# An adaLN block with memory attention and a gated FFN: deferred steps placed by an emission clock, and a new order of loads, Wo and norms

## The chip, the cores and the metric

The kernel runs on one core of a Trainium2 chip. The metric is device time in microseconds (us) of one execution; the time of a kernel is the median of its runs. A core has TensorE (PE in the profile: matmuls and transposes, which write to PSUM), VectorE (DVE), ScalarE (ACT), GpSimd (POOL) and SyncE (SP). Each works through its own instructions in program order, and an instruction waits on semaphores until what it reads is there and the buffer that it writes is free. Transfers are issued from the queues of SP and ACT and are carried out by 16 DMA engines that all queues share.

## The reference

The input x is 2048 tokens by 448, in bf16. A conditioning row c gives six rows of modulation, each 448 long. With the constants written out, what is computed is

```python
mod = silu(c) @ w_mod                      # sa, ca, ga, sb, cb, gb
h = layernorm(x) * (1 + ca) + sa
x = x + ga * attn(h)                       # 16 heads of 28, then @ wo
h = layernorm(x) * (1 + cb) + sb
x = x + gb * ((sigmoid(h @ w_gate) * (h @ w_up)) @ w_down)   # 1792 wide
```

The attention goes over the tokens in four segments of 512. Inside a segment it is causal softmax attention. Beside it stands a memory: with phi(t) = t + 1 for t > 0 and exp(t) otherwise, the output of a head is (1 - g) times the softmax result plus g times phi(q) M / (phi(q) z), where M and z sum phi(k) v and phi(k) over all earlier segments, and g is the sigmoid of a learnt number for each head. The first segment has no memory.

## The kernel before

A segment has four tiles of 128 tokens. Heads are handled in four groups of four (`hc`), and a *unit* is one segment and one group. `logits` (L370) computes a unit's transposed logits in three steps (`g` = 0, 1, 2), with an exponential on ACT and a causal mask on POOL behind each; `pv` (L395) multiplies with v and, from the second segment on, with the memory, and combines the two on DVE and POOL; `otr` (L441) transposes the result by DMA. Everything else is *fill*: jobs put between these steps to keep TensorE busy.

The order of all instructions is written out by hand, in one Python program; nothing is reordered later. The main loop (L583) goes over segments, groups and steps. After each `logits`, `run_fill` (L520) takes jobs from the queue `fill` until their listed costs, in ns of TensorE at full clock (a matmul of 512 columns counts 216, of 448 columns 190), reach a quota. What a job overspends is carried as debt.

The jobs are: q, k and v projections (`proj_qk` L308, `proj_v` L319); `mem_k` (L341: phi of k and a DMA transpose to `pk`) and `mem_update` (L350: 16 matmuls and the new memory); `wo_tile` (L450: output projection of a tile, the residual, and LN2's statistics); `modulate` of LN2 (L259); `gate_up` (L466), 14 for each segment; `down` (L481), four for each segment; and the preparations `prep_b1` to `prep_b3` (L528), which multiply ga into wo and gb into w_down on POOL and compute the second norm's modulation columns.

Steps that need another engine to finish first are deferred: `later(n, fn)` emits fn after n *ticks*, and a tick is one job or one attention step, whatever its length (L73 to L88). phi (L330) puts its exponential on ACT at once and its two DVE operations two ticks later. A layer norm of a segment (`class LN`, L232) runs statistics on DVE, a power on POOL, the normalisation on DVE, four DMA transposes from SP and four modulations on DVE. For segment 0 the transposes are done by TensorE (`pe_chunk`, L264), and the modulation takes the data out of PSUM. For LN1 of segments 1 to 3 its steps are jobs of cost 0, blended one by one between the projections of the segment before (`ln1_jobs` L277, `blend` L289).

SP carries the loads of x, of most modulation matrices, wq, wv and wo, all DMA transposes and the stores. ACT's queue carries the loads of w_gate, w_up and w_down, blended between the projections of segment 0 (`ffn_load_jobs` L146). POOL clears the unused rows of wo, w_gate and w_up at the beginning (`late_loads` L132). A tile of PSUM for matmul results comes from a ring of four banks (`ps_m`); the logits have the other four.

When segment s - 1's last `otr` is out (segment s, group 0), the four `wo_tile` jobs of s - 1 are put in front of the fill, and behind it `down` of s - 2, the modulations of LN2 and the gate/up jobs of s - 1 (L594 to L600). The last segment's gate, up and down run at the end with nothing to interleave.

## Time and profile before

| | us |
|---|---|
| median of three runs | 325.17 (323.58 to 325.18) |
| profiled execution, its own time | 324.38 |
| its span, first to last instruction | 322.4 |
| TensorE busy | 267.0 (83% of the span) |
| VectorE busy | 184.2 (57%) |
| ScalarE busy | 141.7 (44%) |
| GpSimd busy | 105.9 (33%) |
| mean granted TensorE clock | 0.91 of full speed |

Times in the profile count from the first instruction. A busy TensorE is not a fast one: its clock is granted between half and full speed, and four matmuls of 512 columns take 0.86 us at full clock, so the same work is longer where the clock is low. In a row of the timeline, the bracket at the end is the idle time of the engine just before the instruction and what ended it. A line number such as L261 is that of the kernel before; a helper has one line for all who call it.

### The profile page before, as it was taken

The page shows a single profiled execution, that of the slowest core. Times are in us where ns is not written, and L with a number is a line of the kernel's source. Part 1 is how long each engine was busy: PE and PEld are TensorE (multiplying, and loading weights), DVE is VectorE, ACT ScalarE, POOL GpSimd, SP SyncE. Part 2 cuts the span into 40 slices and gives each one's busy share as a digit, 9 for nine tenths or more (in the row PEclk, how much of TensorE's full clock was granted, in tenths as well). Part 3 has the DMA queues.
Part 4 walks back from the last instruction along what each step waited for, and adds up shares of the span by engine and source line. Part 5 has one row for each costly group of instructions (what it writes and reads, how often), then busy time and mean ns, then how long its engine had stood idle before and what let it go on. Part 6 is the DMA issues. An engine that isn't in the chain of part 4 may idle for free.

```text
span 322.4 us, 5232 instructions
## 1 busy us (share of the span) xinstructions
PE 267.0 (83%) x2032; PEld 126.3 (39%) x2032; DVE 184.2 (57%) x403; ACT 141.7 (44%) x171; POOL 105.9 (33%) x162
## 2 busy tenths in 40 slices
PE   6679029959779639999599599989959999989996
PEld 2424004516334303445145154435514554534452
DVE  4846365489496952763484455469562754743421
ACT  1237305855866505576603357763436521023310
POOL 0808100636359780322443030435431310400000
PEclk9969657989999957999679799999968999999999
DMA  6978990234631110000012100001310001210001
GB/s 172 290 167 259 229 234 9 50 78 88 116 67 36 42 40 0 18 2 16 18 44 64 33 16 3 16 18 33 95 31 2 16 2 32 63 47 0 0 16 43
DMA packets 43088, 20.18 MB, mean 63 GB/s; under 512 B 31800, under 2 KB 42168, under 8 KB 43064
## 3 DMA queue, kind: packets, MB, share of 16 engines
q1 hardware_dynamic: 39016, 14.01, 19.6%
q10 hardware_dynamic: 4048, 5.85, 5.9%
q8 instruction: 16, 0.26, 0.3%
q14 instruction: 8, 0.07, 0.1%
HBM read 10.67 MB, written 1.84 MB: 39 GB/s over the span
## 4 chain that ended last, share of the span: by engine, by line
PE 52%; DVE 23%; DMA 9%; ACT 6%; POOL 5%; issue 3%; SPq 1%; POOLq 0%; ACTq 0%; DVEq 0%
PE gps L471 14%; PE ups L476 14%; PE dps L484 11%; ACT pT L386 5%; DMA hT<-xn 5%; PE pq L312 4%; DVE xn L250 4%; DVE hT L261 3%; PE acc L405 3%; DVE st L242 3%; PE lg L383 3%; PE pwo L453 3%; DMA pk<-pkt 2%; DVE e L335 2%; DVE pkt L336 2%
## 5 line engine op out<-in xcount | busy, mean ns | idle before, releaser
L386 ACT ACTIVATE pT<-lg 128x2048 bf16<-128x2048 f32 (+1 forms) x48 | 76.5, 1593 | 56.9 <-PE lg L383 54.4
L471 PE MATMUL gps<-hT,wg_sb 128*128 128x512 bf16 x224 | 63.5, 400 | 14.9 <-DVE hT L261 14.1
L479 DVE SCALAR_TENSOR_TENSOR fT<-tt,ups 128x512 bf16<-128x512 f32 x56 | 38.4, 686 | 61.6 <-PE ups L476 45.7
L392 POOL TENSOR_SCALAR_AFFINE_SELECT pT<-pT 128x512 bf16<-128x512 bf16 x64 | 39.9, 641 | 69.8 <-ACT pT L386 66.3
L473 ACT ACTIVATE tt<-gps 128x512 f32<-128x512 f32 x56 | 32.8, 596 | 67.1 <-PE gps L471 67.1
L476 PE MATMUL ups<-hT,wu_sb 128*128 128x512 bf16 x224 | 60.3, 393 | 0.0
L484 PE MATMUL dps<-wd_sb,fT 128*128 128x448 bf16 x224 | 44.4, 354 | 0.0
L471 PEld LDWEIGHTS <-wg_sb 128*128 128x128 bf16 x224 | 20.8, 100 | 43.9 <-issue 17.1
L312 PE MATMUL pq<-hT,wq_sb 128*128 128x512 bf16 x64 | 20.8, 437 | 18.8 <-DVE hT L261 18.8
L476 PEld LDWEIGHTS <-wu_sb 128*128 128x128 bf16 x224 | 22.5, 101 | 29.8 <-issue 5.4
L439 POOL TENSOR_TENSOR ou<-t,t 128x448 bf16<-128x448 f32 x12 | 13.8, 1147 | 60.1 <-DVE t L438 52.7
L484 PEld LDWEIGHTS <-fT 128*128 128x128 bf16 x224 | 21.7, 98 | 21.0 <-issue 1.5
L383 PE MATMUL lg<-qT,kT 28*128 28x512 bf16 (+3 forms) x256 | 17.9, 312 | 5.6 <-ACT pT L386 4.2
L261 DVE TENSOR_SCALAR hT<-hT,cols 128x512 bf16<-128x512 bf16 x28 | 14.5, 564 | 12.6 <-DMA hT<-xn 12.6
L488 DVE TENSOR_TENSOR ot<-dps,x_sb 128x448 bf16<-128x448 f32 x16 | 10.0, 622 | 19.8 <-PE dps L484 18.8
L250 DVE TENSOR_SCALAR xn<-x_sb,mv,rs 128x448 bf16<-128x448 bf16 x32 | 16.8, 545 | 6.5 <-POOL rs L247 6.5
L242 DVE BATCH_NORM_STATS2 st<-x_sb 128x6 f32<-128x448 bf16 x32 | 19.7, 617 | 1.3 <-DMA x_sb<-in_A_x_dram 0.7
L312 PE MATMUL pq<-hT,wk_sb 128*128 128x512 bf16 x64 | 19.3, 430 | 0.9 <-DVE kT L317 0.9
L405 PEld LDWEIGHTS <-pT 128*128 128x128 bf16 x640 | 18.3, 96 | 4.0 <-issue 0.8
L405 PE MATMUL acc<-vt,pT 128*128 128x29 bf16 x640 | 18.5, 175 | 0.6 <-ACT qT L315 0.6
L541 POOL TENSOR_TENSOR wd_sb<-wd_sb,gb 128x448 bf16<-128x448 bf16 x14 | 15.4, 1111 | 6.4 <-ACT gb L225 6.4
L453 PE MATMUL pwo<-wo_sb,oT 128*128 128x448 bf16 x64 | 16.1, 409 | 0.9 <-DMA oT<-ou 0.8
(82 smaller groups left out, 251.9 us busy)
## 6 DMA issues: line engine op xcount, KB each, us to landing
wm<-in_w_mod_dram SPq DMA_DIRECT2D x5, 392.0 KB, 4.9
out_dram<-ot SPq DMA_DIRECT2D x16, 112.0 KB, 1.7
wd_sb<-in_B_w_down_dram ACTq DMA_DIRECT2D x1, 1568.0 KB
x_sb<-in_A_x_dram SPq DMA_DIRECT2D x3, 448.0 KB, 6.1
wg_sb<-in_B_w_gate_dram ACTq DMA_DIRECT2D x3, 448.0 KB, 4.0
wu_sb<-in_B_w_up_dram ACTq DMA_DIRECT2D x3, 448.0 KB, 6.7
hT<-xn SPq DMA_TRANSPOSE x28, 2.3
wm<-in_w_mod_dram ACTq DMA_DIRECT2D x1, 392.0 KB, 6.3
```

The lines of the kernel that those rows point to most:

```text
L242: nc.vector.bn_stats(st[:], self.srcs[i])
L250: nc.vector.tensor_scalar(self.xn[:, i, 0:D], self.srcs[i], self.mv[:, i, 0:1], self.rs[:, i:i + 1], op0=ALU.subtract, op1=ALU.mult)
L312: nc.tensor.matmul(pq[:, 0:L], lhsT=head_cols(w_sb, k, hc), rhs=h[:, k, :], start=(k == 0), stop=(k == NK - 1))
L383: nc.tensor.matmul(lg[:, hs, wid:wid + nq], lhsT=kT[r, hc, kb * P:(kb + 1) * P], rhs=qT[r, hc, kb * P:L], start=True, stop=True, tile_posi ...
L386: nc.scalar.activation(pT[:, :, w0:w0 + wid], lg[:, :, 0:wid], AF.Exp, scale=scale)
L392: nc.gpsimd.affine_select(out=blk, in_=blk, compare_op=ALU.is_ge, fill=0.0, base=0, pattern=[[0, 4], [1, P]], channel_multiplier=-1)
L405: nc.tensor.matmul(accv[:, qb, hs, 0:ME], lhsT=pT[:, hs, c0:c0 + P], rhs=vt[:, kb, hc * 4 + hs, 0:ME], start=(kb == 0), stop=(kb == qb))
L471: nc.tensor.matmul(gp[:, 0:L], lhsT=wg_sb[:, k, fs], rhs=h[:, k, :], start=(k == 0), stop=(k == NK - 1))
L473: nc.scalar.activation(tt[:], gp[:, 0:L], AF.Tanh, scale=0.5)
L476: nc.tensor.matmul(up[:, 0:L], lhsT=wu_sb[:, k, fs], rhs=h[:, k, :], start=(k == 0), stop=(k == NK - 1))
L479: nc.vector.scalar_tensor_tensor(ft[:], tt[:], 1.0, up[:, 0:L], op0=ALU.add, op1=ALU.mult)
L484: nc.tensor.matmul(dp[:, 0:D], lhsT=fT_of[(s, fc)][:, t * P:(t + 1) * P], rhs=wd_sb[:, fc, :], start=(fc == 0), stop=(fc == NFC - 1))
```

## The change

Five things are changed together.

1. `later` takes a time in ns and a tag. A clock counts the listed costs of all that is emitted; a deferred step is emitted when the clock has passed its time. `need(tag)` emits all steps of that tag at once, where something that reads them is emitted. The attention steps tick 450 (logits) and 1100 (`pv`).
2. LN1 of segments 1 to 3 is one job that defers its steps: statistics 900 ns apart, the power at 3600, normalisations from 5200, modulations from 13500. LN1 of segment 1 is started ahead of the first projection and transposed by TensorE, all four chunks evicted by DVE. `mem_k` is spread over 1300 ns steps, phi's DVE part comes 2000 or 3500 ns after its exponential.
3. Loads: all on SP; x of segments 1 and 2 early; beta and the third modulation matrix behind them; wo, x of segment 3, the fourth modulation matrix and w_gate behind segment 0's projections; w_up in segment 1's, w_down ahead of segment 2's. The clearing of wo, w_gate and w_up goes from POOL to DVE, ahead of the loads in the program; two of four pad copies of wk go from POOL to DVE. The modulation matrices get a padded row, so that `mod_cols` needs two evictions in place of four.
4. Order: the first five units take 2500 ns of fill per step, the others an equal share of what is left; debt goes on over segments. `wo_tile` jobs still come at group 1 of the next segment; behind them the rest of the fill; then three `down` tiles, the modulations of LN2 as one job, the fourth `down` tile and the gate/up jobs. For segment 0 `prep_b3` stands behind the second gate/up job. The memory update stands behind the first eight projections of the next segment (four in segment 3), where it was six.
5. The end: two of the last `down` tiles are put in the fill ahead of Wo of the last segment, two behind.

```diff
-    def later(n, fn):
-        deferred.append([n, fn])
...
+    def later(ns, fn, tag):
+        deferred.append((clock[0] + ns, len(deferred), fn, tag))
...
+    def tick(ns):
+        clock[0] += ns
+        run_deferred(lambda d: d[0] <= clock[0])
+
+    def need(*tags):
...
+            run_deferred(lambda d: d[3] == tag)
...
+    wm_bufs = [wts.tile([KP, NK * D + DP - D], BF16, name=f"wm{i}") for i in range(2)]
...
+    for b in wm_bufs:
+        nc.vector.memset(b[:, NK * D:], 0.0)
+    nc.vector.memset(wo_sb[:], 0.0)
+    nc.vector.memset(wg_sb[LW:P, 3, :], 0.0)
+    nc.vector.memset(wu_sb[LW:P, 3, :], 0.0)
...
-        nc.gpsimd.memset(wo_sb[:], 0.0)
...
-        nc.gpsimd.memset(wg_sb[LW:P, 3, :], 0.0)
-        nc.gpsimd.memset(wu_sb[LW:P, 3, :], 0.0)
-
-    def ffn_load_jobs():
...
+    def ln1_start(s, by_pe=False):
+        def start():
+            ln = ln1_of[s] = LN([x_sb[:, s * TPS + t, :] for t in range(TPS)], ("1", s))
+            tag = ("ln1", s)
+            for t in range(TPS):
+                later(900 * t, lambda t=t: ln.stats(t), tag)
+            later(3600, lambda: ln.rstd(0, TPS), tag)
+            for t in range(TPS):
+                later(5200 + 500 * t, lambda t=t: ln.norm(t) if by_pe else ln.norm_t(t), tag)
+            if not by_pe:
+                for kc in range(NK):
+                    later(13500 + 500 * kc, lambda kc=kc: ln.modulate(kc, 0), tag)
+        return (0, start)
+
+    def ln1_pe_jobs(s):
+        def job(kc):
+            need(("ln1", s))
+            ln1_of[s].pe_chunk(kc, 0, False)
+        return [(4 * TR, lambda kc=kc: job(kc)) for kc in range(NK)]
...
-        later(2, lambda: ln.norm_t(t))
+        later(1500, lambda: ln.norm_t(t), ("ln2", s))
...
-        return [(0, lambda kc=kc: ln2_of[s].modulate(kc, 2)) for kc in range(NK)]
+        def mods():
+            need(("ln2", s))
+            for kc in range(NK):
+                ln2_of[s].modulate(kc, 2)
+        return [(0, mods)]
...
-        pad_copy(nc.gpsimd if k < 2 else nc.vector, wk_sb, wk_st, k)
+        pad_copy(nc.vector, wk_sb, wk_st, k)
     mod_cols(((0, 0), (1, 1)))
-    late_loads()
+    load_x(nc.sync, TPS, 2 * TPS)
+    load_x(nc.sync, 2 * TPS, 3 * TPS)
+    ln1_start(1, True)[1]()
...
+    fill.extend(sp(load_bw2) + j0[2:6] + sp(late_consts) + m[0][0:1] + j0[6:])
+    fill.extend(sp(load_wo) + sp(load_wm3) + [ln1_start(2)] + load_ffn(wg_sb, B_w_gate))
+    fill.extend(ln1_pe_jobs(1) + j1[:8] + load_ffn(wu_sb, B_w_up) + m[0][1:] + m[1][0:1] + j1[8:] + [(1000, prep_b1)])
+    fill.extend([ln1_start(3)] + sp(load_wd) + j2[:8] + m[1][1:] + m[2][0:1] + [(2000, prep_b2)] + j2[8:])
+    fill.extend(j3[:4] + m[2][1:] + j3[4:])
...
-    quota = total / 48.0
-
+    early = 2500.0
+    rate = lambda s, hc: early if s * NHC + hc < 5 else (total - 15 * early) / 33.0
...
+                if s >= 1 and hc == 1 and g == 0:
+                    gj = gu_jobs(s - 1)
+                    tail = list(fill)
+                    fill.clear()
+                    fill.extend(wo_jobs(s - 1) + tail)
+                    if s >= 2:
+                        dj = down_jobs(s - 2)
+                        fill.extend(dj[:3] + h2_jobs(s - 1) + dj[3:] + gj)
+                    else:
+                        fill.extend(h2_jobs(s - 1) + gj[:2] + [(1000, prep_b3)] + gj[2:])
+                debt = run_fill(rate(s, hc) + debt)
...
-                    if hc == 0:
-                        fill.extendleft(reversed(wo_jobs(s - 1)))
-                        if s >= 2:
-                            fill.extend(down_jobs(s - 2))
-                        fill.extend(h2_jobs(s - 1) + gu_jobs(s - 1))
...
+    fill.extend(dj[:2])
+    run_fill(3000)
+    for c, fn in wo_jobs(last):
         fn()
-        tick()
+        tick(c)
+    fill.extend(dj[2:])
     run_fill(1e9)
```

149 lines of the change are left out of this document (68 added, 81 removed).

## The prediction

> **What bounds the kernel now.** I read four views in this order: the share of each engine on the page, the busy time by stretch, the waits of TensorE, and the timeline around each wait. PE, DVE, ACT and POOL are TensorE, VectorE, ScalarE and GpSimd.
>
> ```profile
> PE 267.0 (83%) x2032; PEld 126.3 (39%) x2032; DVE 184.2 (57%) x403; ACT 141.7 (44%) x171; POOL 105.9 (33%) x162
> ```
> ```profile
> 18.24:117.27 99.03, 69.03 (x597) 32.49 (x596) 64.06 (x140) 53.80 (x69) 47.00 (x70) 0.86 0.47 110
> 117.27:322.40 205.13, 186.69 (x1364) 88.02 (x1364) 107.71 (x232) 83.80 (x96) 50.90 (x79) 0.93 0.10 25
> ```
> ```profile
> 32.50:47.20 14.70, 1.24 (x3) 0.29 (x4) 6.54 (x16) 3.26 (x6) 0.66 (x2) 0.60 0.98 242
> 47.20:53.30 6.10, 6.10 (x26) 2.00 (x26) 3.73 (x10) 3.02 (x3) 0.63 (x1) 0.57 0.11 22
> 70.30:86.80 16.50, 15.15 (x154) 7.80 (x153) 13.23 (x30) 10.73 (x15) 10.39 (x13) 0.92 0.55 110
> 91.00:107.00 16.00, 14.47 (x166) 8.02 (x165) 13.03 (x22) 10.30 (x12) 14.83 (x17) 1.00 0.24 51
> 117.27:123.80 6.53, 5.60 (x13) 1.65 (x14) 3.33 (x4) 0.60 (x1) 3.53 (x4) 0.50 0.00 0
> 155.20:164.50 9.30, 7.13 (x25) 2.48 (x25) 4.84 (x12) 3.64 (x4) 4.97 (x9) 0.50 0.07 16
> 181.78:186.00 4.22, 4.22 (x12) 1.55 (x12) 1.28 (x3) 0.60 (x1) 0.00 (x0) 0.60 0.01 4
> 237.05:244.00 6.95, 6.29 (x18) 1.75 (x18) 3.05 (x4) 1.76 (x3) 2.85 (x4) 0.53 0.08 19
> ```
>
> Each row of the second and third fence is a stretch in us, its length, the busy us of PE, PE's weight loads, DVE, ACT and POOL, the granted clock, the DMA share and GB/s. TensorE bounds the program, but not evenly. I cut it where the first q projection starts (18.24) and where the first gate matmul starts (117.27), and call the three parts A, B and C. B holds all projections and memory updates; PE is idle there for 99.03 - 69.03 = 30.0 us. C is gate, up and down with the later attention; PE is idle for 18.4 us. Behind each long gap the clock stands at 0.50 to 0.60 for four to seven us, so a gap is paid twice. The gaps have two main owners:
>
> ```profile
> PE pq L312 <- DVE hT L261: 18.8, 8, 11.8
> PE gps L471 <- DVE hT L261: 14.1, 8, 5.3
> ```
>
> Both are layer norms arriving late: LN1 ahead of a segment's projections, LN2 ahead of its gate/up matmuls.
>
> **The change, part by part.** The emission order of the new code can be worked out by adding job costs; I give its positions in us of that emission clock, zero at the first q projection.
>
> *Part A, 18.24 us.*
>
> ```profile
> 1.28 0.24 DVE L125 MEMSET wq_sb<- 64x224 uint32 x1
> 2.81 7.93 PE L547 MATMUL warm<-qT,ident 128*128 128x512 bf16 x24 [2.81 <-DVE qT L176]
> 6.12 0.63 DVE L242 BATCH_NORM_STATS2 st<-x_sb 128x6 f32<-128x448 bf16 x1 [0.75 <-DMA x_sb<-in_A_x_dram]
> 10.58 1.26 PE L209 MATMUL cp<-silu,wm 112*128 112x1 bf16 x32
> 10.63 4.47 DVE L250 TENSOR_SCALAR xn<-x_sb,mv,rs 128x448 bf16<-128x448 bf16 x4 [1.49 <-POOL rs L247]
> 15.03 1.91 DVE L558 COPY wk_sb<-wd_sb 128x448 bf16<-128x448 bf16 x2
> 16.87 0.32 DVE L217 COPY cols<-cp 64x4 f32<-64x4 f32 x2
> 18.24 1.87 PE L312 MATMUL pq<-hT,wq_sb 128*128 128x512 bf16 x4
> 32.59 1.61 DVE L250 TENSOR_SCALAR xn<-x_sb,mv,rs 128x448 bf16<-128x448 bf16 x4 [1.99 <-POOL rs L247]
> ```
> ```profile
> L261 DVE TENSOR_SCALAR hT<-hT,cols 128x512 bf16<-128x512 bf16 x28 | 14.5, 564 | 12.6 <-DMA hT<-xn 12.6
> L274 DVE TENSOR_SCALAR hT<-lntr,cols 128x512 bf16<-128x512 bf16 x2 | 1.0, 537 | 0.1
> ```
>
> Three large memsets (wo_sb, wg_sb, wu_sb, 896 words a partition each) move to DVE ahead of the warm-up's operand. At 0.24 us for 224 words they cost about 0.96 each, 2.9 in all with two small pads beside. The warm-up starts near 5.8 instead of 2.81 and ends near 13.7; the 32 column matmuls end near 15.0. Against that, POOL no longer works during the first norms: four took 4.47 us beside POOL's copies and memsets, and 1.61 without. DVE is through them at 12.3. Two wk copies come over from POOL. No full copy on a quiet POOL stands in the trace; the bounds are 0 and the 1.91 that two of them took beside POOL's memset. I take 0.4 each, a norm of the same tile, so 1.6: done by 13.9, under the column matmuls. At 1.91 each they end near 20, and q starts near 21. Two column evictions instead of four (0.32) end at 15.3, the first hT eviction (L274, 0.54) at 15.9, and the last of the transposes ahead of q by 16.5. Part A: -1.7, bounds -2 and +3. DVE's wait for x, until 6.12, hides the memsets from the norm; the warm-up and the column matmuls behind it do move by 2.9, which is in these sums.
>
> *Part B, 99.03 us.* The large gap:
>
> ```profile
> 33.32 5.36 SPq L257 DMA_TRANSPOSE hT<-xn  x4
> 44.25 0.61 PE L312 MATMUL pq<-hT,wq_sb 128*128 128x512 bf16 x1 [11.76 <-DVE hT L261]
> ```
>
> Segment 1's norm is normalised at 32.6 because its statistics stand between projection jobs, then goes through four DMA transposes that share the 16 DMA engines with the weights (0.98 busy, 242 GB/s). The change starts its statistics ahead of the first projection and transposes on PE: 16 small matmuls and four evictions from PSUM on DVE. These replace four DMA transposes and four in-place modulations (L261, 0.56; the evictions 0.54 by L274); nothing of it waits for the DMA. PE gains 1 to 2 us of work, DVE nothing worth counting. The 11.76 us gap, the smaller gaps behind it, and the cold 6.1 us after it go. What is late next is DVE: its work stays about 64 us (63.5 after the scaling of wd, which slows it, has left), against about 64 us for PE at full clock (69.03 less some 5 for the cold matmuls, of which 47.20:53.30 alone gives 6.10 x 0.43 = 2.6). Neither runs at 100% in B: in the two densest stretches above DVE is 13.23 / 16.5 = 0.80 and 13.03 / 16 = 0.81 busy, PE 0.92 and 0.90. So B lasts 63.5 / 0.81 = 78 us. Bounds: 64 / 0.92 = 70 if PE sets it, and 98 if DVE keeps today's pace of 64.06 / 99.03 = 0.65. I take 78, since DVE is the engine nearer to its limit there. Part B: -21, bounds -29 and -1.
>
> The weights change queue as well. Gate, up and down leave ACT's queue, whose sequencer issued nine transfers, and go to SP's as five, into the line of the DMA transposes.
>
> ```profile
> wo_sb<-in_A_wo_dram SPq DMA_DIRECT2D x4, 98.0 KB
> wg_sb<-in_B_w_gate_dram ACTq DMA_DIRECT2D x3, 448.0 KB, 4.0
> wm<-in_w_mod_dram SPq DMA_DIRECT2D x5, 392.0 KB, 4.9
> ```
> ```profile
> L257 SPq DMA_TRANSPOSE hT<-xn x28: 1188/1190/2075, 33.3 to 281.2; - x28
> DMA to landing us min/median/max: 2.3/2.3/6.2
> ```
>
> Wo (4 x 98 KB), x of segment 3 (448 by its shape), the fourth modulation matrix (392) and gate (3.5 x 448) are issued right behind the third pk transpose, at about 11.5 of the clock, near 30 us. That is 2800 KB, 2.87 MB, or 11.8 us at 242 GB/s. Behind them on SP stand the last pk transpose, segment 2's four hT transposes and oT; then up (1568 KB, 6.6 us) ahead of three pk; then down (6.6 us) ahead of the fourth pk and segment 3's hT. The memory update that needs pk is at 22.1, or 16.5 + 22.1 x 78 / 63.7 = 43.5 us; the loads are through at 30 + 11.8 = 42. The modulations of segment 2 are due at 25.3 (47.5 us), those of segment 3 at 42.6 (68.7). Each has a few us. I add nothing here; transposes landed in 2.3 to 6.2 us even beside a full DMA. What it costs when that cover is gone is the first rival.
>
> The Trainium skill, DMA: Bandwidth & Descriptors, section on queues, rings and completion order, speaks against this move: SP and ACT each own one ring per DMA engine, descriptors of a ring start in order, and an engine takes turns between rings. By it a transpose that used to be interleaved with ACT's weights now waits for all weights issued ahead of it, and the sum would be the first rival's. No run here shows it yet, since today's weights and transposes stand on different queues.
>
> *Part C, 205.13 us.* The end of each gap is a matmul:
>
> ```profile
> 155.47 0.40 PE L383 MATMUL lg<-qT,kT 28*128 28x256 bf16 x4 [1.98 <-ACT pT L386]
> 159.63 5.03 PE L453 MATMUL pwo<-wo_sb,oT 128*128 128x448 bf16 x13 [0.78 <-DMA oT<-ou]
> 181.78 0.38 PE L471 MATMUL gps<-hT,wg_sb 128*128 128x512 bf16 x1 [2.85 <-DVE hT L261]
> 215.96 0.40 PE L383 MATMUL lg<-qT,kT 28*128 28x512 bf16 x4 [1.13 <-ACT pT L386]
> 237.05 0.59 PE L471 MATMUL gps<-hT,wg_sb 128*128 128x512 bf16 x1 [2.76 <-DVE hT L261]
> ```
> ```profile
> 219.74 2.65 PE dps L484 x14
> 240.05 1.71 PE ups L476 x4
> 244.69 0.86 PE gps L471 x4
> ```
> ```profile
> L541 POOL TENSOR_TENSOR wd_sb<-wd_sb,gb 128x448 bf16<-128x448 bf16 x14 | 15.4, 1111 | 6.4 <-ACT gb L225 6.4
> ```
>
> (1) The first gates run cold: 117.27:123.80 holds 13 matmuls, which at 0.86 for four take 2.8 us instead of 6.53. In the new order eight projection jobs and a unit of attention stand between Wo and them, so no long gap is in front: -3.5. (2) Around 155 the filling work has run out, because the debt of each segment is dropped and Wo comes only after oT. The new rate spends the 14 gate/up jobs exactly up to the next segment's second unit, and three of them lie between the last PV and Wo. 155.20:164.50 (9.3 us) holds work of about 3.5 us (16 Wo matmuls, of which 13 take 5.03 at half clock, are 3.1; logits 0.4): -5.8, and I leave 1.1 for oT: -4.7. (3) Before segment 1's and 2's gates, the modulations stood right in front of the gate jobs. Now one down tile (2.65 us) stands between. DVE still has an output normalisation and phi before them, as today: at 237 the whole gap of 2.76 was these and the modulations' start. Nearly all of it is now under the down tile; I leave 1.2 for the modulations, which follow at 0.56 each while a gate matmul takes 0.22. Gap plus cold: 2.85 + 1.5 (12 matmuls in 4.22, warm 2.6) and 2.76 + 3.6 (18 in 6.95, of which 4 are logits: warm 3.3); less 1.2 each: -3 and -5. (4) The gap of 1.13 at 215.96 closes: -1. (5) The gb replication moves here with the 14 POOL multiplications (1.11 each, 15.4 us): +0.9 on PE; POOL is busy 50.90 of 205.13 us in C and has room. Nothing in the last segment is moved that ends anything: its modulations still wait for the last down tile.
>
> Part C: -17.2 + 0.9 = -16.3; bounds -19 and -8, the latter if (3) stays as it is.
>
> The sum: 322.4 - 1.7 - 21.0 - 16.3 = 283.4 us of span. The profiled execution took 324.38 at that span, so 2.0 around it: 285.4. The median of the runs shown, 325.17, is 0.8 above the profiled one: 286.
>
> **The rivals.** *Transposes held by the weights.* For: SP's queue is in order, and from 30 us on it holds 25.0 us of loads (11.8 + 6.6 + 6.6) and 15 transposes up to segment 3's last hT, at 1.19 us of issue 18 us. If these follow one another, that hT lands at 30 + 43 + 2.3 = 75.3, 6.6 late, and the first memory update is some 3 late: +10, 296. Against: issue and transfer overlap today. *DVE keeps its pace of 0.65 in B*, the deferred work being only spread differently: 98 for B, 306. Against: the two dense stretches. *The modulations are as late as before* (norm chains on DVE before them): part C gives 8, 294. *Slower:* DMA transposes on SP's one queue are served one at a time, each only after the previous has landed, once weights are in the same queue. Segment 3's modulations then start after the 15, and 21.1 / 63.7 of B, 26 us, still follow. The gains of A and C are used up when B lasts 99 + 18 = 117 us and the first gate starts at 133.5, so it decides from (133.5 - 26 - 30) / 15 = 5.2 us each; at the 6.2 us seen under load the gate starts at 149 instead of 94.5, and the time is 286 + 54 = 340. Against: the four at 33.32 were issued 1.34 us apart and overlapped under 242 GB/s.
>
> **How the numbers follow.** The forecast 0.60 (its own range 275 to 296), held transposes 0.15 (296), late modulations 0.07 (294), DVE's pace 0.11 (306), slower 0.05 (340), and 0.02 for that last one near its break-even. The low end is B near 68 with the rest as computed, or B at 70 and C at its bound, 274; the high end reaches nearly to DVE's pace, 305. Less than 0.5% is about what a measurement of this kernel cannot tell from no change; that is the 0.02. Slower is 0.05, faster the other 0.93.
>
> **What would show it.** Right: the first q at 16 to 17; no wait of PE on hT longer than 3 us; the first gate between 86 and 102; no clock at 0.5 after the warm-up. Wrong: PE's memory update or q of segment 2 waiting on a pk or hT transpose issued behind gate, up or down (first rival); DVE below 0.7 in B without a DMA wait (second); a gap near 2.8 before the gates of segments 1 and 2 (third); transposes landing 5 us apart (fourth). The forecast is wrong if the first gate comes after 105.

## The result and the profile after

The changed kernel takes 293.4 us (median of four runs, 291.12 to 294.63); the kernel before took 325.05 beside it. The ratio is 0.9031, with a 95% interval from 0.897 to 0.9092. The forecast was 286 us, its range 274 to 305. The profiled execution took 292.24 us, with a span of 290.2.

The first view is the busy time by stretch of the changed kernel, cut where the prediction cut: at the first q projection and at the first gate matmul. Columns as before: stretch, length, busy us of PE, its weight loads, DVE, ACT and POOL, granted clock, DMA share, GB/s. The line ahead of them is the page's own, with the engines' shares.

```profile
PE 257.2 (89%) x2048; PEld 124.2 (43%) x2048; DVE 186.5 (64%) x405; ACT 140.4 (48%) x171; POOL 101.7 (35%) x157
...
0.00:14.50 14.50, 8.57 (x72) 4.54 (x73) 10.17 (x37) 3.92 (x7) 2.02 (x9) 1.00 0.86 231
14.50:97.13 82.63, 68.93 (x612) 32.90 (x612) 64.79 (x138) 54.88 (x70) 38.10 (x60) 0.92 0.57 135
97.13:290.20 193.07, 179.73 (x1364) 86.72 (x1364) 111.55 (x232) 81.56 (x95) 61.56 (x88) 0.98 0.11 26
```

Part A went from 18.24 to 14.50 (-3.7, forecast -1.7), part B from 99.03 to 82.63 (-16.4, forecast -21.0), part C from 205.13 to 193.07 (-12.1, forecast -16.3). The span is 32.2 us shorter, where 39.0 were forecast. PE's busy time fell from 267.0 to 257.2 us with 16 matmuls more, since the clock is higher (0.965 in the mean, 0.91 before). In eight later kernels whose instructions up to the first q are the same, that point lies between 14.26 and 15.50, so a difference of one us in A means nothing; two of them that also leave B alone (e2, e8) have a B of 84.3 and 84.5, so two us in B mean nothing either. One execution of the later run e5 took 864.61 us and is left out of its figures.

The waits of PE in the changed kernel (in all, times, longest):

```profile
PE dM L357 <- DMA pk<-pkt: 6.3, 3, 2.4
PE gps L474 <- DVE hT L257: 5.6, 5, 2.7
PE dps L488 <- DVE fT L482: 2.5, 3, 1.3
PE pq L311 <- DVE hT L270: 1.9, 1, 1.9
```

The two old owners, 18.8 us on hT ahead of q and 14.1 ahead of the gates, are down to 1.9 and 5.6. New are the waits of all three memory updates on pk and of down tiles on fT. The timeline at two memory updates and at the gates of segment 1, then SP's queue (its second column is how long the issue took), and then three stretches behind such waits by busy time:

```profile
45.65 0.39 PE L357 MATMUL dM<-vt,pk 128*128 128x116 bf16 x4 [2.40 <-DMA pk<-pkt]
65.15 0.39 PE L357 MATMUL dM<-vt,pk 128*128 128x116 bf16 x4 [1.90 <-DMA pk<-pkt]
153.96 0.38 PE L474 MATMUL gps<-hT,wg_sb 128*128 128x512 bf16 x1 [2.72 <-DVE hT L257]
```
```profile
35.06 0.49 SPq L130 DMA_DIRECT2D wg_sb<-in_B_w_gate_dram  x1
36.22 1.56 SPq L346 DMA_TRANSPOSE pk<-pkt  x1
56.97 0.53 SPq L597 DMA_DIRECT2D wd_sb<-in_B_w_down_dram  x1
57.60 3.09 SPq L346 DMA_TRANSPOSE pk<-pkt  x1
```
```profile
66.60:72.00 5.40, 5.40 (x65) 2.85 (x62) 3.40 (x7) 3.90 (x6) 1.39 (x2) 0.68 0.70 136
97.13:103.00 5.87, 5.87 (x65) 3.00 (x66) 3.21 (x9) 1.46 (x2) 0.00 (x0) 0.71 0.05 11
153.96:160.00 6.04, 5.52 (x16) 1.89 (x15) 2.77 (x5) 1.19 (x2) 1.08 (x2) 0.72 0.16 41
```

The last pk transpose of segment 0 is issued at 36.22, right behind w_gate, and its reader starts at 45.65: over 9 us. That of segment 1 stands right behind w_down. In the last fence the clock behind waits of 1.90, 1.35 and 2.72 us is 0.68 to 0.72, so here these waits are paid twice. It isn't so each time: in e2 and e8 the first gate stands behind the same wait, 1.37 us, and the clock of the 5.9 us behind it is 1.00.

### The profile page after: what moved, and what is told of

It reads as the page before. It is cut to its first block, busy times and chain, and to the rows that moved or that the text cites. A ratio compares the mean times of both kernels' runs of the same rounds, so it can differ in the third digit from the quotient of the medians.

```text
span 290.2 us, 5243 instructions
## 1 busy us (share of the span) xinstructions
PE 257.2 (89%) x2048; PEld 124.2 (43%) x2048; DVE 186.5 (64%) x405; ACT 140.4 (48%) x171; POOL 101.7 (35%) x157
## 4 chain that ended last, share of the span: by engine, by line
PE 48%; DVE 27%; DMA 9%; ACT 6%; POOL 4%; issue 4%; SPq 1%; DVEq 0%; ACTq 0%
PE gps L474 14%; PE ups L479 14%; PE dps L488 9%; DMA pk<-pkt 7%; ACT pT L387 4%; DVE st L238 4%; DVE e L335 3%; PE acc L406 3%; DVE x_sb L459 3%; PE lg L384 3%; PE warm L553 2%; DVE pkt L336 2%; DVE xn L246 2%; POOL wd_sb L547 1%; DVE pqt L336 1%
## 5 line engine op out<-in xcount | busy, mean ns | idle before, releaser
L474 PE MATMUL gps<-hT,wg_sb 128*128 128x512 bf16 x224 | 60.0, 387 | 5.6 <-DVE hT L257 5.6
L393 POOL TENSOR_SCALAR_AFFINE_SELECT pT<-pT 128x512 bf16<-128x512 bf16 x64 | 44.0, 702 | 52.5 <-ACT pT L387 52.2
L479 PE MATMUL ups<-hT,wu_sb 128*128 128x512 bf16 x224 | 59.3, 388 | 1.3 <-DVE t L434 1.2
L406 PEld LDWEIGHTS <-pT 128*128 128x128 bf16 x640 | 18.9, 98 | 5.0 <-issue 2.4
L311 PE MATMUL pq<-hT,wq_sb 128*128 128x512 bf16 x64 | 17.5, 383 | 2.5 <-DVE hT L270 1.9
L246 DVE TENSOR_SCALAR xn<-x_sb,mv,rs 128x448 bf16<-128x448 bf16 x32 | 15.3, 502 | 6.3 <-POOL rs L243 6.3
L323 PE MATMUL pv<-wv_sb,hT 128*128 128x448 bf16 x64 | 16.3, 401 | 2.5 <-DVE kT L316 2.1
L311 PE MATMUL pq<-hT,wk_sb 128*128 128x512 bf16 x64 | 17.1, 392 | 0.0
L456 PE MATMUL pwo<-wo_sb,oT 128*128 128x448 bf16 x64 | 15.2, 386 | 0.5 <-DMA oT<-ou 0.5
L242 POOL TENSOR_SCALAR rs<-mv 128x1 f32<-128x1 f32 (+1 forms) x20 | 4.9, 244 | 27.1 <-DVE mv L239 27.0
```

The source lines that it names most:

```text
L246: nc.vector.tensor_scalar(self.xn[:, i, 0:D], self.srcs[i], self.mv[:, i, 0:1], self.rs[:, i:i + 1], op0=ALU.subtract, op1=ALU.mult)
L311: nc.tensor.matmul(pq[:, 0:L], lhsT=head_cols(w_sb, k, hc), rhs=h[:, k, :], start=(k == 0), stop=(k == NK - 1))
L393: nc.gpsimd.affine_select(out=blk, in_=blk, compare_op=ALU.is_ge, fill=0.0, base=0, pattern=[[0, 4], [1, P]], channel_multiplier=-1)
L406: nc.tensor.matmul(accv[:, qb, hs, 0:ME], lhsT=pT[:, hs, c0:c0 + P], rhs=vt[:, kb, hc * 4 + hs, 0:ME], start=(kb == 0), stop=(kb == qb))
L474: nc.tensor.matmul(gp[:, 0:L], lhsT=wg_sb[:, k, fs], rhs=h[:, k, :], start=(k == 0), stop=(k == NK - 1))
L479: nc.tensor.matmul(up[:, 0:L], lhsT=wu_sb[:, k, fs], rhs=h[:, k, :], start=(k == 0), stop=(k == NK - 1))
```

## The experiments

Times are medians; ratios are to the kernel before, measured in the same session, with their 95% interval. The changed kernel's own is 0.9031 (0.897 to 0.9092).

**e1: the weights back on ACT's queue.**

```diff
-        return sp(lambda: load_w(nc.sync, w_sb, w))
+        return sp(lambda: load_w(nc.scalar, w_sb, w))
...
-        nc.sync.dma_start(wd_sb[:], B_w_down...)
+        nc.scalar.dma_start(wd_sb[:], B_w_down...)
```

> The changed kernel with gate, up and down loaded from ACT's queue again, at the same places of the order; nothing else differs. Theory (transposes held behind weights on SP's queue): the memory updates wait 2.40, 1.90 and 2.01 us on pk in the changed kernel; with SP's queue free of 4.5 MB the first two go below 0.7, the last pk transpose of segments 0 and 1 lands within 4 us of its issue instead of 7.5, and with the cold matmuls behind the gaps part B falls from 82.6 to 77-80 us: 288 to 291 us. Rival (the pk chain is late because DVE and POOL are late, or the 16 DMA engines are full whichever queue fills them): the waits stay within 0.7 us of where they are, 292 to 295 us. A second rival: ACT, whose sequencer must issue the loads, holds exps and q evictions up; then PE waits on ACT in B and the time rises by 1 to 3 us.

Measured: 294.11 us, ratio 0.907 (0.9026 to 0.9114). PE's waits up to the first gate, and the transposes of that stretch (the number at the end is the median us from issue to landing; it was 2.5 for pk in the changed kernel):

```profile
PE pq L311 <- DVE hT L257: 4.7, 4, 2.6
PE dM L357 <- DMA pk<-pkt: 2.3, 2, 2.0
```
```profile
pk<-pkt SPq DMA_TRANSPOSE x12, 4.4
```
```profile
53.06 2.91 DVE L257 TENSOR_SCALAR hT<-hT,cols 128x512 bf16<-128x512 bf16 x4 [3.75 <-DMA hT<-xn]
```

The mechanism of the theory is real: the first two waits on pk are nearly gone, 2.3 us are left of 6.3. Its price is not: 4.7 us on segment 2's hT have taken their place. The last row shows DVE waiting 3.75 us there for a DMA transpose, where it waits for none in the changed kernel (49.97), and the pk transposes land later too. The rule that the prediction cites (the Trainium skill, DMA: Bandwidth & Descriptors, section on queues, rings and completion order) fits the waits on pk: 6.3 us with the weights ahead of the transposes in one ring, 2.3 with the weights in the other. That a second queue makes the kernel faster doesn't follow here.

**e6: the weights later.** w_gate moves behind the first memory update, w_up to w_down's old place, w_down behind the third memory update.

```diff
-    fill.extend(... + [ln1_start(2)] + load_ffn(wg_sb, B_w_gate))
+    fill.extend(... + [ln1_start(2)])
-    ... j1[:8] + load_ffn(wu_sb, B_w_up) + m[0][1:] + m[1][0:1] + j1[8:] ...
+    ... j1[:8] + m[0][1:] + m[1][0:1] + load_ffn(wg_sb, B_w_gate) + j1[8:] + load_ffn(wu_sb, B_w_up) ...
-    fill.extend([ln1_start(3)] + sp(load_wd) + j2[:8] ...)
+    fill.extend([ln1_start(3)] + j2[:8] ...)
-    fill.extend(j3[:4] + m[2][1:] + j3[4:])
+    fill.extend(j3[:4] + m[2][1:] + sp(load_wd) + j3[4:])
```

> The changed kernel with gate, up and down still on SP's queue but each issued later: gate behind the first memory update instead of ahead of segment 1's projections, up at the place of down's old issue, down behind segment 2's memory update. With the loads on ACT's queue the memory updates' waits went from 6.3 to 2.3 us but waits of 3.8 us on hT of segment 2 came in their place, so the queue is not it. Theory (the 16 DMA engines are full from 30 to 60 us, whichever queue fills them, and transposes land late for that): the first two waits on pk go below 1 us, no wait on hT of segment 2 takes their place, the first gate starts at 92 to 95 us, 288 to 291 us. Rival (the loads only hold up other transposes, or DVE is late by itself): waits of PE on DMA and hT ahead of 97 us stay at 5 us or more in all, 292 to 295 us.

Measured: 294.12 us, ratio 0.9067 (0.9027 to 0.9108). The first gate starts at 99.29.

```profile
56.83 1.21 PE L406 MATMUL acc<-vt,pT 128*128 128x29 bf16 x40 [2.59 <-DVE kT L316]
99.29 1.03 PE L474 MATMUL gps<-hT,wg_sb 128*128 128x512 bf16 x2 [3.88 <-DVE hT L257]
```

Again the first two waits on pk go (none, and 0.79) and others come: 2.59 on a kT eviction, and 3.88 ahead of the first gates, where w_down now is in transit beside LN2's transposes. The rival's number holds. The weights did leave room: from 34 to 50 us the DMA engines are busy for 0.64 of the time instead of 1.00, and PE works all 16.0 us instead of 13.6. By the first gate that lead is gone. So full DMA engines can explain the first two waits, but not by themselves the length of B.

**e7: the evictions of kT on ACT.**

```diff
-            jobs.append((4 * MM, lambda hc=hc: proj_qk(s, hc, wk_sb, kT_of[s], "dve")))
+            jobs.append((4 * MM, lambda hc=hc: proj_qk(s, hc, wk_sb, kT_of[s], "act")))
```

> The changed kernel with the 16 evictions of kT (0.68 us each) on ACT instead of DVE, so that DVE has some 9 to 10 us less in part B (64.8 of 82.6 us) and ACT as much more (54.9). Theory of the prediction (DVE sets the length of B at 0.8 of its time): B falls by 5 to 10 us, 284 to 289 us. Rival (B is set by latencies of chains and by the DMA engines, not by the amount of work on DVE): B changes by under 2.5 us, 291 to 295 us; if ACT's exps are held up by the evictions, above that.

Measured: 293.04 us, ratio 0.9038 (0.8992 to 0.9085). Part B of this kernel:

```profile
14.56:98.11 83.55, 69.03 (x612) 33.22 (x612) 54.49 (x122) 62.30 (x86) 37.54 (x60) 0.92 0.62 134
```

DVE has 10.3 us less to do in B, 0.65 of its time, and B is 83.55 us long. How much work DVE has does not set B by itself. ACT has 7.4 us more to do, but PE waits only 1.8 us on ACT in B. The waits on DVE's kT are gone, and others have grown: those on pk from 6.3 to 7.9 us, the one ahead of the first gate from 1.35 to 3.13.

**e9: each memory update four projection jobs later.**

```diff
-    ... j1[:8] + load_ffn(wu_sb, B_w_up) + m[0][1:] + m[1][0:1] + j1[8:] + [(1000, prep_b1)])
+    ... j1[:8] + load_ffn(wu_sb, B_w_up) + j1[8:] + m[0][1:] + m[1][0:1] + [(1000, prep_b1)])
-    ... j2[:8] + m[1][1:] + m[2][0:1] + [(2000, prep_b2)] + j2[8:])
+    ... j2[:8] + [(2000, prep_b2)] + j2[8:] + m[1][1:] + m[2][0:1])
-    fill.extend(j3[:4] + m[2][1:] + j3[4:])
+    fill.extend(j3[:8] + m[2][1:] + j3[8:])
```

> The changed kernel with each of the three memory updates four projection jobs (3 us of PE) later in the order, with the start of the next segment's pk chain behind it; nothing else moves. Moving loads to the other queue, loading later, and 10 us less work on DVE left part B where it was, and each time PE waited 2 to 8 us at the memory updates or at the tile that DVE, held by a transpose, made late. Theory (the position of the memory update in the order is what PE waits for; the last pk lands 2 to 3 us after PE asks): the three waits on pk fall from 6.3 us to below 2 in all, the first gate starts at 90 to 94 us, 287 to 290 us. Rival (B is set by the chain of transposes through DVE as a whole, so the wait moves to pv, acc or hT): the first gate starts after 95.5 us, 291.5 to 295 us.

Measured: 298.63 us, ratio 0.9198 (0.9155 to 0.9242): slower than the changed kernel, and outside the ranges of both expectations. The trace is that of an execution of 301.57 us; the others took 297.31 to 301.44. SP's queue, DVE and PE:

```profile
49.57 0.67 SPq L597 DMA_DIRECT2D wd_sb<-in_B_w_down_dram  x1
54.48 4.61 SPq L346 DMA_TRANSPOSE pk<-pkt  x1
```
```profile
63.77 0.73 DVE L336 SCALAR_TENSOR_TENSOR pkt<-kT,e 128x512 bf16<-128x512 bf16 x1 [3.18 <-DMA pk<-pkt]
73.64 1.83 DVE L257 TENSOR_SCALAR hT<-hT,cols 128x512 bf16<-128x512 bf16 x3 [6.58 <-DMA hT<-xn]
```
```profile
66.08 4.33 PE L323 MATMUL pv<-wv_sb,hT 128*128 128x448 bf16 x12 [3.94 <-DVE kT L316]
```

The waits on pk are gone from PE, as the theory said, and the first gate starts at 106.36 all the same, which is the rival's sign. In B, PE now waits 5.7 us on kT, 4.5 on segment 2's hT and 3.5 on oT. The edit did more than move the reader: it started segment 1's pk chain later, and without the memory update in between w_down's load came 7.4 us earlier (49.57 instead of 56.97), two us behind w_up. The pk transposes stand behind both; DVE then waits 3.18 us for one of the three buffers of phi, which are free only when their transpose has landed, and behind that 6.58 us for hT. Evictions that are ready, such as kT's, stand behind the first of these waits, and PE waits for them (3.94 us in the last row). So taking the reader away doesn't take the chain of transposes through DVE away. That the short waits in the changed kernel are a mild form of it is likely by these rows, but not shown: this edit moved a load as well.

**e4: segment 1's LN1 as early, but by DMA transposes.**

```diff
-    ln1_start(1, True)[1]()
+    ln1_start(1)[1]()
-    fill.extend(ln1_pe_jobs(1) + j1[:8] + ...)
+    fill.extend(j1[:8] + ...)
```

> The changed kernel with segment 1's LN1 started as early, but transposed by four DMA transposes on SP's queue and modulated in place on DVE, as the other segments' are; no PE transposes for it. Theory A (the early start alone removes the 11.76 us gap): hT of segment 1 is there before its q projection, PE is spared 16 small matmuls, 291 to 294 us. Theory B (the DMA path is what was late, since the transposes share the DMA engines and SP's queue with wo, x, wm and gate): PE waits 3 us or more for hT ahead of segment 1's q, 297 to 305 us.

Measured: 304.39 us, ratio 0.9378 (0.9332 to 0.9424), first gate at 105.92.

```profile
32.32 1.89 PE L311 MATMUL pq<-hT,wq_sb 128*128 128x512 bf16 x4 [3.40 <-DVE hT L257]
60.48 0.59 PE L311 MATMUL pq<-hT,wq_sb 128*128 128x512 bf16 x1 [2.67 <-DVE hT L257]
165.71 2.29 PE L474 MATMUL gps<-hT,wg_sb 128*128 128x512 bf16 x4 [4.71 <-DVE hT L257]
```

Theory B's numbers hold, and the PE transposes are worth 0.035 of 325, 11 us, in the changed kernel. Only 1.5 of these are at segment 1's q (3.40 instead of 1.85 us). The rest is further on: segment 2's hT is late (2.67, with 0.80 and 1.09 at its first two chunks), and the gaps ahead of the gates are longer (2.65 instead of 1.35, 4.71 instead of 2.72). Why the last of these grew, 130 us after the edit, isn't explained by what was run.

**e5: the kernel before, with the early LN1 and its PE transposes alone.**

```diff
-            if kc % 2:
+            if kc % 2 and self.key[1] == 0:
...
+    def ln1_early(s):
+        ln = LN([x_sb[:, s * TPS + t, :] for t in range(TPS)], ("1", s))
+        for t in range(TPS):
+            ln.stats(t)
+        ln.rstd(0, TPS)
+        norms = [(0, lambda t=t: ln.norm(t)) for t in range(TPS)]
+        return norms + [(0, lambda: None)] * 13, [(240, lambda kc=kc: ln.pe_chunk(kc, 0)) for kc in range(NK)]
...
-    fill.extend(blend(blend(... + m[0][0:4], ln1_jobs(1), 1), ffn_load_jobs(), 3, 2))
-    fill.extend(blend(j1[:6] + ...))
+    norms1, chunks1 = ln1_early(1)
+    fill.extend(blend(blend(... + m[0][0:4], norms1, 1), ffn_load_jobs(), 3, 2))
+    fill.extend(blend(chunks1 + j1[:6] + ...))
```

> The kernel before with one part of the change alone: the statistics of segment 1's LN1 are issued ahead of the remaining projection jobs, and its hT comes from 16 PE transposes with evictions on DVE; weights stay on ACT's queue, the rest of the order, the quota and the memsets stay. Theory (that gap and the cold clock behind it were most of part B's loss): the 11.76 us wait ahead of segment 1's q goes, the matmuls behind it are no longer cold, first gate at 101 to 105 us instead of 117.27, 309 to 314 us. Rival (the gap only closes to open again at the next late tile, the memory update on pk or segment 2's hT): first gate after 108 us, 316 to 322 us.

> The kernel before with segment 1's LN1 early and by PE transposes, once more, for a trace: timed, it was 0.994 of the kernel before, though the 11.76 us wait should be gone. Theory (the gap opens again further on): the first gate starts at 114 to 118 us, and waits of PE of 8 us or more in all stand ahead of it on pk, on hT of segment 2 or 3, or on Wo's oT, which the kernel before doesn't have. Rival (the gap was never closed, since the chunks are late too): a wait of over 6 us on hT or lntr at 30 to 45 us.

Measured: 322.98 us (nine executions), ratio 0.994 (0.9907 to 0.9974). The trace is that of a second run of the same kernel, e5b, a single execution of 325.12 us. Its DVE and PE:

```profile
38.81 0.29 DVE L343 TENSOR_SCALAR e<-e 128x512 bf16<-128x512 bf16 x1 [5.68 <-ACT e L340]
...
45.91 0.69 DVE L344 SCALAR_TENSOR_TENSOR pkt<-kT,e 128x512 bf16<-128x512 bf16 x1 [4.02 <-DMA pk<-pkt]
...
47.27 0.51 DVE L274 TENSOR_SCALAR hT<-lntr,cols 128x512 bf16<-128x512 bf16 x1
```
```profile
47.84 0.59 PE L320 MATMUL pq<-hT,wq_sb 128*128 128x512 bf16 x1 [8.83 <-DVE hT L274]
```

The first theory falls. Of its rival only the late first gate came, at 126.55. The theory of e5b's expectation falls too, and its rival holds: the gap isn't closed. PE has transposed, but the evictions stand on DVE behind all four phi of segment 0. These wait 5.68 us for ACT's exponentials, and the last waits 4.02 us for a buffer that a pk transpose still reads, while the weights fill the DMA engines. With the old order a tile that PE has transposed waits for the DMA after all, by way of DVE's program order. In this trace part B is 108.08 us, 9 longer than before (99.03), and part C 196.65, 8.5 shorter (205.13); why C is shorter was not run.

**e13: e5, and the first memory chain spread as the change spreads it.** Three phi start among the projections of segment 0, the fourth goes behind the PE transposes.

```diff
-    ... j0[4:] + m[0][0:4], norms1, 1) ...
+    ... j0[4:6] + m[0][0:1] + j0[6:8] + m[0][1:2] + j0[8:10] + m[0][2:3] + j0[10:], norms1, 1) ...
-    fill.extend(blend(chunks1 + j1[:6] + ...))
+    fill.extend(blend(chunks1 + m[0][3:4] + j1[:6] + ...))
```

> The kernel before with segment 1's LN1 early and by PE transposes, as in the run that gained 0.6%, and beside it the first memory chain spread: the phi of heads group 0, 1 and 2 start among the projections of segment 0, and that of group 3 behind the four PE transposes. In that run the four evictions of hT stood on DVE behind all four phi, the last of which waited 4.02 us for one of three buffers that a pk transpose held, while ACT's weights filled the DMA engines. Theory (the PE transposes pay only when their evictions do not stand behind that chain): PE's wait of 8.83 us on hT falls below 2.5, its q projection starts at 37 to 41 us instead of 47.84, 310 to 317 us. Rival (PE is held by the same chain a few jobs later, or the exponentials and weights are what is late): the first gate stays after 114 us, 319 to 324 us.

Measured: 315.0 us, ratio 0.9684 (0.9645 to 0.9723).

```profile
37.83 0.51 DVE L274 TENSOR_SCALAR hT<-lntr,cols 128x512 bf16<-128x512 bf16 x1
```
```profile
38.39 0.38 PE L320 MATMUL pq<-hT,wq_sb 128*128 128x512 bf16 x1 [0.50 <-DVE hT L274]
116.95 1.87 PE L479 MATMUL gps<-hT,wg_sb 128*128 128x512 bf16 x4 [8.33 <-DVE hT L261]
```

The theory holds where it applies: the evictions start 9.4 us earlier (37.83 instead of 47.27), the q projection too, and the time is in its range. Of the rival one number holds as well, a first gate after 114 us: it starts at 116.95, as before the change (117.27), because PE now waits 8.33 us on LN2's modulations ahead of it, a wait that e5 has too, where the kernel before has 5.30. Part B is 98.55 us, 9.5 less than in e5 and no less than before; part C is 196.55, as in e5. So the spread chain takes 9.5 us out of B once the transposes are PE's. Against the kernel before, the gap at segment 1's q is closed and B is as long, and the gain of 10 us stands in C. The spread chain was not run alone.

**e3: memsets and two wk copies back on POOL.**

```diff
-    nc.vector.memset(wo_sb[:], 0.0)
-    nc.vector.memset(wg_sb[LW:P, 3, :], 0.0)
-    nc.vector.memset(wu_sb[LW:P, 3, :], 0.0)
...
-    pad_copy(nc.vector, wk_sb, wk_st, k)
+    pad_copy(nc.gpsimd if k < 2 else nc.vector, wk_sb, wk_st, k)
...
+    nc.gpsimd.memset(wo_sb[:], 0.0)
+    nc.gpsimd.memset(wg_sb[LW:P, 3, :], 0.0)
+    nc.gpsimd.memset(wu_sb[LW:P, 3, :], 0.0)
```

> The changed kernel with the memsets of wo_sb, wg_sb and wu_sb and two of the four wk copies back on POOL, where the kernel before had them. Theory (part A gained because POOL no longer slows DVE's norms and copies): the four norms take 3 us or more again instead of 1.32, first q projection at 17.5 to 18.5 us instead of 14.50, 296 to 297.5 us. Rival (A gained from the merged column evictions and from the loads, not from the memsets): first q at 14 to 15.5 us, 292 to 294 us. The memsets leave DVE, so the warm-up starts some 2.5 us earlier in both.

Measured: 298.53 us, ratio 0.9164 (0.9113 to 0.9216), first q at 17.90. DVE and POOL of this kernel, and then DVE and PE of the changed one:

```profile
10.74 4.48 DVE L243 TENSOR_SCALAR xn<-x_sb,mv,rs 128x448 bf16<-128x448 bf16 x4 [1.49 <-POOL rs L240]
15.14 1.92 DVE L561 COPY wk_sb<-wd_sb 128x448 bf16<-128x448 bf16 x2
11.71 1.71 POOL L567 MEMSET wo_sb<- 128x1792 bf16 x1
```
```profile
10.55 1.32 DVE L246 TENSOR_SCALAR xn<-x_sb,mv,rs 128x448 bf16<-128x448 bf16 x4 [1.49 <-POOL rs L243]
11.78 0.82 DVE L564 COPY wk_sb<-wd_sb 128x448 bf16<-128x448 bf16 x4
```
```profile
5.87 6.87 PE L553 MATMUL warm<-qT,ident 128*128 128x512 bf16 x24 [5.87 <-DVE th L177]
```

The theory holds, in its start of q if not quite in its time: beside POOL the four norms take 4.48 us instead of 1.32, and a copy 0.96 instead of 0.21, so the first q is 3.4 us later. The whole is 0.013 of 325, 4 us, slower.

**e2: LN2's modulations after two down tiles instead of three.**

```diff
-                        fill.extend(dj[:3] + h2_jobs(s - 1) + dj[3:] + gj)
+                        fill.extend(dj[:2] + h2_jobs(s - 1) + dj[2:] + gj)
```

> The changed kernel with the LN2 modulations of segments 1 and 2 placed after two down tiles of the earlier segment instead of three, so that two down tiles (5.3 us of PE) stand between them and the first gate instead of one. Theory (in segment 1 an output normalisation and a slow phi stood ahead of the modulations on DVE, so one down tile was too little cover): the gap of 2.72 us ahead of segment 1's gates falls below 0.7, the stretch behind it is not cold any more, part C falls by 3 to 4.5 us: 289 to 291 us. Rival (the modulations end as late as before because they then wait on DVE for the last hT transpose, and the output normalisation queued behind them makes the oT or the PV late): a wait of 1 us or more appears on oT, acc or the gates, and the time stays within 1.5 us of 293.4.

Measured: 289.6 us, ratio 0.8933 (0.8891 to 0.8974). DVE of the changed kernel, then of e2, then the clock of e2 at that place:

```profile
151.74 1.53 DVE L336 SCALAR_TENSOR_TENSOR pqt<-qT,e 128x512 bf16<-128x512 bf16 x1
153.19 1.99 DVE L257 TENSOR_SCALAR hT<-hT,cols 128x512 bf16<-128x512 bf16 x3
```
```profile
149.40 1.38 DVE L257 TENSOR_SCALAR hT<-hT,cols 128x512 bf16<-128x512 bf16 x4 [1.85 <-DMA hT<-xn]
```
```profile
152.00:158.00 6.00, 4.51 (x22) 1.66 (x21) 5.03 (x10) 2.25 (x4) 3.35 (x4) 1.00 0.20 58
```

In the changed kernel the modulations start at 153.19, behind an output normalisation and a phi. In e2 they wait 1.85 us for the transpose and are still 3.8 us earlier; the gates start at 151.38 without a wait of their own, at full clock, and part C falls from 193.07 to 188.36 us. Of these 4.7 us, 1.2 are not the edit's: from the first gate to the logits in front of Wo, ahead of all that it moves, the changed kernel takes 34.06 us, with a clock of 0.71 over the first 5.87, and e2 takes 32.85, with a clock of 1.00 over the first 5.86. The rival is half right: the output normalisation now is late, and an up matmul waits 1.27 us, but that is the smaller price.

**e8: the two left-over gate/up jobs ahead of Wo, in the last segment.**

```diff
-                    fill.extend(wo_jobs(s - 1) + tail)
+                    fill.extend(tail + wo_jobs(s - 1) if s == 3 else wo_jobs(s - 1) + tail)
```

> The changed kernel with one move in the last segment's order: the two gate/up jobs left over from segment 1 come ahead of the four Wo tiles of segment 2 instead of between them and segment 1's first down tile. Theory (a wait that the change made: the down tile needs the last two fT, whose DVE operations stand behind the LN2 chain of the Wo tiles): the waits of 1.33 and 0.36 us on fT at 195 to 198 us and 1.17 us on a PSUM bank at 190 go, LN2 of segment 2 still has three down tiles as cover, 290 to 292 us. Rival (the LN2 chain then is late in its turn): a wait of over 1 us ahead of segment 2's gates, 293 us or more.

Measured: 290.81 us, ratio 0.8943 (0.8902 to 0.8985). The same 16 us of the changed kernel and of e8:

```profile
182.00:198.00 16.00, 13.14 (x115) 6.06 (x114) 13.37 (x29) 6.83 (x7) 7.77 (x14) 1.00 0.14 32
```
```profile
182.00:198.00 16.00, 15.64 (x130) 7.74 (x128) 11.38 (x28) 9.26 (x9) 6.76 (x14) 1.00 0.10 23
```

The theory holds: PE works 15.64 of 16 us instead of 13.14, and part C falls to 189.22 us. Of these 3.9 us, 1.2 lie ahead of the edit as in e2 (32.86 us to the logits in front of the first Wo). Each of e2 and e8 is faster than both kernels, than the changed one by 0.010 and 0.009 in the ratio, little more than the intervals allow; both edits in one kernel were not run.

**e12: Wo, LN2's modulations and down at their old places.**

```diff
-                if s >= 1 and hc == 1 and g == 0:
...
-                    fill.extend(wo_jobs(s - 1) + tail)
...
-                        fill.extend(dj[:3] + h2_jobs(s - 1) + dj[3:] + gj)
...
                 if prev[0] >= 0 and g == 2:
                     otr(*prev)
+                    if hc == 0:
+                        gj = gu_jobs(s - 1)
+                        fill.extendleft(reversed(wo_jobs(s - 1)))
+                        if s >= 2:
+                            fill.extend(down_jobs(s - 2) + h2_jobs(s - 1) + gj)
+                        else:
+                            fill.extend(h2_jobs(s - 1) + gj[:2] + [(1000, prep_b3)] + gj[2:])
```

> The changed kernel with the old places of Wo, the LN2 modulations and the down tiles in part C: Wo in front of the remaining work right behind the first oT transpose of the next segment, the down tiles of the earlier segment ahead of the modulations, and the modulations right in front of the gates. Rate, debt, loads and LN1 stay as changed. Theory of the prediction (these places and the debt gave part C its gain of 12 us): C takes 199 to 205 us instead of 193, with a wait over 2 us ahead of segment 2's gates as well, 299 to 305 us. Rival (C gained because no segment runs dry and its stretches are not cold, whatever the order of Wo): C takes 192 to 196 us, 292 to 296 us.

Measured: 294.27 us, ratio 0.9071 (0.9039 to 0.9103); part C 194.1 us. PE ahead of the gates of segments 1 and 2:

```profile
156.74 0.38 PE L474 MATMUL gps<-hT,wg_sb 128*128 128x512 bf16 x1 [3.02 <-DVE hT L257]
...
211.46 1.34 PE L474 MATMUL gps<-hT,wg_sb 128*128 128x512 bf16 x4 [0.71 <-DVE hT L257]
```

The rival holds. With the modulations right in front of the gates again, segment 2's gap is 0.71 us, not the 2.76 of the kernel before. The new places are worth about one us, which these runs can't tell from nothing.

## Why the prediction was right and wrong

**The sign and the range were right**, and so were two signs named for it: the first gate at 97.13 (86 to 102) and no wait on hT over 3 us. The sign that failed is the clock: the 5.87 us behind the first gate average 0.71, but in them the clock from 99 to 101 us is 0.50. The first q came earlier (14.50 for 16 to 17). Of the forecast gains, A brought 2.0 us more, B 4.6 and C 4.2 less; the span is 6.8 us longer than the 283.4 worked out.

**Part A, too small.** The reason was right (e3), and the start of the warm-up (5.87, forecast 5.8). What was mis-sized lies behind it: the 24 warm-up matmuls took 6.87 us instead of the 7.93 carried over from the kernel before, the column matmuls 0.94 instead of 1.26, a wk copy 0.21 instead of 0.4. The granted clock in A is 1.00, where it was 0.91.

**Part B, the model was wrong.** That the 11.76 us gap and its cold stretch go was right. The step that failed is "What is late next is DVE": 63.5 / 0.81 = 78 took a busy share for a limit. With 10.3 us less on DVE, B is as long (e7). That 82.63 lies within the range given for B says nothing for this model. "I add nothing" for the weights on SP's queue failed too, in a way that no case foresaw: the first rival's sign came, 6.3 us on pk behind w_gate and w_down, but taking the weights out of that queue (e1) or moving them later (e6) gave nothing back. What the runs show in its place are chains in program order: a phi on DVE waits for a buffer that a DMA transpose holds, and evictions that PE needs wait behind the phi. e5 and e13 show that for the first memory update, e9 for the second. In the changed kernel PE waits 6.3 us of its 13.7 idle ones (82.63 - 68.93) on pk itself, and each edit that shortened this wait (e1, e6, e9) brought others. Which part of the chain sets the length of B there is not settled, and neither is what the DMA engines have to do with it, whose share from 34 to 66 us is 1.04 by the profile.

The prediction also gave the whole gain of the gap to the early start and the PE transposes. Alone on the kernel before they gave 2 us, and the gap stayed (e5). They need the spread memory chain, which the prediction put down nowhere as a term; with both the gap closes and the gain is 10 us (e13), though B as a whole is no shorter there, as the wait ahead of the first gate has grown.

**Part C, the terms came unevenly.** (2) came: no dry stretch, and Wo waits 0.54 us for oT. (4) came: no wait of logits over 0.3 us is left in C. (5) came as priced: its four matmuls take 0.92 us. (3) came for segment 2 only, and mostly not for the reason given: e12 has the old place and a gap of 0.71. For segment 1 it failed, at "Nearly all of it is now under the down tile": one down tile is 2.65 us, and the gap stayed 2.72, as the third rival had it, because the modulations came behind a normalisation and a phi of 1.53 us; with two tiles as cover it goes (e2). (1) came in part: the clock behind the first gates is 0.71, not full, after a wait of 1.35 us on LN2; with a wait of 1.37 it is full in e2 and e8 and 0.71 in e12, so how much of (1) comes differs from execution to execution. Not foreseen at all were the waits on fT, which the order made by putting segment 1's down tiles right behind its last gate/up jobs; without them C is 3.9 us shorter, 1.2 of it by the clock of the first gates (e8). Each fix alone brings C to 188.4 and 189.2, where 188.8 was forecast.

**What stays open.** Undone one by one in the changed kernel, the PE transposes are worth 11 us, the memsets and copies 4, the places of Wo and LN2 one or none, the weights' queue none. That leaves about 15 of the 31.5 us to the rest: the memory and LN1 chains placed by the emission clock, the rate of the fill, and the debt that goes on over segments. Those were not run by themselves in the changed kernel, so what each is worth is open, and e5 and e13 show that the parts don't add.

## What to carry to other kernels

An operation that is taken off a slow path still waits for whatever stands ahead of it on the engine that takes over its result: look up the program order there, and what those instructions wait for, before the gap is booked as gained. Then see where the time ends up: in e13 a wait of 8.83 us was gone and the first gate started where it had before. A busy share of 0.8 in a dense stretch is no capacity; take some of the work away and see if the time moves. For a step that has a certain latency, count the cover behind its own predecessors on its engine, not behind the place where it is written in the order.

## What the runs showed of the hardware

By an estimate from e1, a DMA transpose occupies the DMA engines well beyond its bytes. In this run the weights alone are on ACT's queue (q10), all else on SP's (q1); the DMA view from 25 to 97 us (72 us), with packets, MB and the share of 16 engines' time:

```profile
q1 hardware_dynamic: 17112, 5.61, 48.5%
q10 hardware_dynamic: 2768, 4.82, 21.2%
...
hT<-xn SPq DMA_TRANSPOSE x11, 3.0
oT<-ou SPq DMA_TRANSPOSE x4, 2.9
```

The weights took 15.3 us of all engines, 315 GB/s. At that rate the 2.06 MB of x, wo and modulation matrices on SP's queue in this stretch take 6.5 of the other 34.9 us, and 28.4 are left for 27 transposes: an estimate of 1.05 us each, where their 131 KB at 315 GB/s would take 0.42. It fits with this that the choice of queue brought nothing. By the same estimate the four that TensorE took over free about 4 us of the engines in a stretch where they are busy 0.98 of the time in the changed kernel:

```profile
31.50:45.60 14.10, 11.48 (x100) 5.24 (x99) 9.50 (x22) 7.47 (x8) 4.12 (x7) 0.88 0.98 235
```

And the granted clock can fall behind gaps shorter than those seen before: it was 0.68 behind the 1.90 us at 65.15 and 0.71 after the 1.35 us at 97.13. It need not: after 1.37 us at the same place it was 0.71 in e12 and 1.00 in e2 and e8. The length of the last gap alone doesn't tell.
